# The last 96 rows of w_down: one load on 16 DMA engines, or on 8 with 12 rows each

## The chip, the cores and the metric

The kernel runs on one NeuronCore of a Trainium2 chip, in one launch. The metric is the device time of one execution in microseconds. The core has TensorE (PE, with its weight loads shown apart as PEld), VectorE (DVE), ScalarE (ACT), GpSimd (POOL) and SyncE (SP), and 16 DMA engines that carry all loads and stores.

## What is computed

A decode step of one token for a batch of B = 2, hidden size D = 512, in float32. The normalised input goes through an attention over the last W = 2048 positions of a cache, and through a bilinear feed-forward part; both are added to the input.

```python
xn = _layernorm(x)                                   # x: (2, 1, 512)
q = (xn @ wq) -> (2, 32, 1, 128)
k, v = k_cache[:, :, Sk - W:], v_cache[:, :, Sk - W:]  # (2, 32, 2048, 128) each
p = softmax(q k^T * 128 ** -0.5)
A = (p v) -> (2, 1, 4096) @ wo                       # wo: (4096, 512)
h = (xn @ w_gate) * (xn @ w_up)                      # F = 1376 columns
Bf = h @ w_down                                      # w_down: (1376, 512)
out = x + A + Bf
```

Almost all of the data is the cache: 32 heads with 2 MB of keys and 2 MB of values each. Every byte is used once.

## The kernel before, in words

**One stream of loads.** The host lays all large inputs out as one long array, `stream`, in the order in which the kernel wants them: keys and values of the heads, and between them the slices of wq, wo, w_gate, w_up and w_down. `blocks()` (from line 40) lists the loads in order, each as a list of fields with their widths; a load fills 128 partitions, each with one contiguous row. `pump()` (lines 148 to 171) issues them all from SP, in that order, into a ring of three large buffers called `step`; it stops when all three are held, and `done()` starts it again when the last field of a buffer has been used. So SP's queue has every large load of the kernel in one fixed order, and the DMA engines run through it.

**Heads.** For each head VectorE multiplies the keys by q (`products`) and adds them up (`sums`); GpSimd takes the maximum and the sum over the partitions; ScalarE takes the exponential; TensorE weighs the values (`pv`, `weigh`), transposes the result and multiplies it by wo (`project_o`), adding it up in a PSUM tile `acc`. Values run three heads behind keys.

**The feed-forward part.** w_gate and w_up come early, and h lies transposed in `hT`. w_down, 1376 rows, is cut into ten chunks of 128 rows and one rest of FR = 96 rows. The chunks are fields `wd` of the stream in four loads, `WD = [(0, 4), (4, 7), (7, 9), (9, 10)]`. The rest isn't in the stream: it is an input of its own, `wd_rest`, and its load is added as the very last of the list (line 142, with `at` None), into the same buffer as the last loads of the stream, on partitions 0 to 95 (line 168).

**The end.** After the last head's values the code calls `transpose(H - 1)`, `down(1)`, `project_o(H - 1)`, `down(2)`, `down(3)` and then the rest, each of the chunks as four matmuls of 128 columns into four row groups of `acc` (`accumulate`). In the profile a float32 matmul stands as two records, so a chunk is x8. Then VectorE adds x (`x_nat`, line 489, tile `o_out`), and SP stores 4 KB.

**Order.** `InOrder` (line 72) ties every instruction to the one before it on its engine, so that each engine runs in the order of the code. Since all calls of PE, DVE, ACT and SP go through it, the profile shows them with one line, L87; tiles tell them apart. `x_nat`, the input in the layout of the output, is loaded at the start from ScalarE's queue by two small loads of 4 rows of 512 bytes each.

Of the kernel before, what the change touches and what calls it, by code (L numbers as in the profile page):

```python
# [16 lines left out]
P = 128  # L17
B, D, H, DH, SK, F = 2, 512, 32, 128, 8192, 1376
# [5 lines left out]
NFC = F // P  # L24
FR = F - NFC * P
# [14 lines left out]
def blocks():  # L40

    def wd(n):
        return [("wd", i, D) for i in range(*WD[n])]

    def k(h):
        first = [("w", 1, CQ - NC * DH)] if h == 0 else []
        return [("k", h, CK)] + first + ([("wq", h, CP)] if h + HG < H else [])

    def v(h):
        return [("v", h, CK), ("wo", h, CO)]

    def gu(half):
        n = NC * (FH[half][1] - FH[half][0])
        return [("wg", half, n), ("wu", half, n)]

    units = []
    for h in range(LAG, H - 1):
        units += [k(h), v(h - LAG)]  # L60
    loads = [k(0), gu(0) + k(1), gu(1) + k(2), units[0] + units[1]]
    loads += [sum(units[i : i + 3], []) for i in range(2, len(units), 3)]
    loads += [k(H - 1) + v(H - 1 - LAG)]
    out = [(("q", 0), [("w", 0, NC * DH)])]
    out += [(("s", i), fields) for i, fields in enumerate(loads)]
    late, last = ("s", len(loads)), ("s", len(loads) + 1)
    out += [(late, v(H - 3)), (late, v(H - 2)), (last, wd(0)), (last, [("v0", H - 1, CK // 2)])]
    out += [(last, [("v1", H - 1, CK // 2), ("wo", H - 1, CO)])]
    return out + [(last, wd(n)) for n in range(1, len(WD))]
# [33 lines left out]
def kernel(  # L103
# [10 lines left out]
    pe, dve, act, sp = (InOrder(tc, e) for e in (nc.tensor, nc.vector, nc.scalar, nc.sync))  # L114
# [28 lines left out]
    tiles, used, left, got = {}, {}, {}, {}  # L143
# [4 lines left out]
    def pump():  # L148
        nonlocal held
        while todo:  # L150
            key, fields, at = todo[0]
            if key not in tiles:
                if key[0] == "q":
                    tiles[key] = const.tile([P, NC * DH], F32, name="wq0")
                elif held == BUFS:
                    return
                else:
                    held += 1
                    tiles[key] = steps.tile([P, STEP], F32, name="step")
                used[key] = 0  # L160
            todo.pop(0)
            c0 = used[key]
            for kind, i, w in fields:
                got[kind, i] = (tiles[key][:, used[key] : used[key] + w], key)
                used[key] += w
            c1 = used[key]
            if at is None:
                sp.dma_start(tiles[key][:FR, c0:c1], wd_rest)
            else:
                src = stream[at : at + P * (c1 - c0)].rearrange("(p i) -> p i", p=P)  # L170
                sp.dma_start(tiles[key][:, c0:c1], src)

    def done(kind, i):
        nonlocal held
        _, key = got.pop((kind, i))
        left[key] -= 1
        if left[key] == 0 and key[0] != "q":
            del tiles[key]
            held -= 1
            pump()  # L180

    pump()

    mean_w = const.tile([P, P], F32, name="mean_w")
# [309 lines left out]
def laid_out(x):  # L494


    import numpy as np

    a = x["A_x"].reshape(B, D)
    xs = a.reshape(B, P, NC).transpose(1, 0, 2).reshape(P, B * NC)  # L500
    picks = np.zeros((P, 4 * B), a.dtype)
    for b in range(B):
        for r in range(4):
            picks[4 * b + r :: 32, r * B + b] = 1.0
    cache = {
        kind: x[name][:, :, SK - W :, :].reshape(B, H, P, J * DH).transpose(1, 2, 0, 3)
        for kind, name in (("k", "A_k_cache"), ("v", "A_v_cache"))
    }
    wq = x["A_wq"].reshape(P, NC, H // HG, GC).transpose(2, 0, 1, 3)
    wo = x["A_wo"].reshape(H, P, D)  # L510
    gu = {
        kind: x[name].reshape(P, NC, F)
        for kind, name in (("wg", "B_w_gate"), ("wu", "B_w_up"))
    }
    wd = x["B_w_down"]

    def field(kind, i):
        if kind in ("k", "v"):
            return cache[kind][i].reshape(P, CK)
        if kind in ("v0", "v1"):  # L520
            return cache["v"][i].reshape(P, B, -1)[:, int(kind[1])]
        if kind == "w":
            return (wq[0][:, :, DH:] if i else wq[0][:, :, :DH]).reshape(P, -1)
        if kind == "wq":
            return wq[i // HG + 1][:, i % HG, :]
        if kind == "wo":
            return wo[i]
        if kind == "wd":
            return wd[i * P : (i + 1) * P]
        return gu[kind][:, :, FH[i][0] : FH[i][1]].reshape(P, -1)  # L530

    parts = [
        np.concatenate([field(kind, i) for kind, i, _ in fields], axis=1).ravel()
        for _, fields in blocks()
    ]
    return {
        "x": xs, "picks": picks, "x_rows": a.reshape(B, D // P, P),
        "stream": np.concatenate(parts), "wd_rest": wd[NFC * P :],
    }


# [29 lines left out]
```

## Time and profile before

| | us |
|---|---|
| median of 3 runs (380.22 to 380.51) | 380.46 |
| the profiled execution, its own time | 380.54 |
| its span, from the first to the last instruction | 378.4 |
| busy: PE / PEld / DVE / ACT / POOL | 260.7 / 93.1 / 294.4 / 63.9 / 25.4 |
| mean granted TensorE clock | 0.815 |

The profile is one execution. A row of a timeline is start, length, engine, line, operation, tiles, and in brackets the idle time of the engine before it and what ended it. SPq is SP's queue: a DMA stands there when it is issued, not when it lands. In a table of stretches the "DMA share" is the mean busy share of the 16 DMA engines; it can pass 1.00, as packets overlap a little.

### The profile page before, as it was taken

The numbers are of one execution on the slowest core, as the hardware profiler recorded it, in microseconds if no ns is written. First come the engines' busy times: TensorE is split into PE (matmuls) and PEld (weight loads), VectorE is DVE, ScalarE is ACT, GpSimd is POOL, SyncE is SP. The second block draws the span as 40 slices with busy tenths as digits, with TensorE's granted clock in tenths as the row PEclk, the third lists the DMA queues.
The fourth block names the chain that finished last, engine by engine and source line by source line (L and its number), as shares of the span: only waits on it lengthen the run. The fifth ranks groups of instructions, "written<-read, shape, count | busy, mean of one in ns | idle before, by whom it ended". The sixth has DMA issues, their size and how long they took to land.

```text
span 378.4 us, 3087 instructions
## 1 busy us (share of the span) xinstructions
PE 260.7 (69%) x1188; PEld 93.1 (25%) x1188; DVE 294.4 (78%) x145; ACT 63.9 (17%) x264; POOL 25.4 (7%) x78
## 2 busy tenths in 40 slices
PE   3939861746848875584885678487667847719996
PEld 3512220212212221221222122122212211204343
DVE  3739892996799499589949959994994999699920
ACT  1020020102102220201222021021112102212221
POOL 0000000000000000000000000000000010000000
PEclk9987995969876696978679588788867869668999
DMA  8999999999999999999999999999999999999994
GB/s 312 456 416 441 421 456 444 409 450 433 413 450 415 444 444 405 450 456 392 457 428 415 456 409 440 456 393 462 444 398 452 415 427 433 445 424 411 431 414 163
DMA packets 5049, 159.65 MB, mean 422 GB/s; under 512 B 828, under 2 KB 844, under 8 KB 1452
## 3 DMA queue, kind: packets, MB, share of 16 engines
q1 hardware_dynamic: 4732, 159.46, 98.2%
q8 instruction: 9, 0.15, 0.2%
q10 hardware_dynamic: 304, 0.01, 0.0%
q14 instruction: 4, 0.03, 0.0%
HBM read 159.46 MB, written 0.00 MB: 421 GB/s over the span
## 4 chain that ended last, share of the span: by engine, by line
DMA 60%; DVE 24%; PE 12%; ACT 2%; SPq 1%; issue 1%; POOL 0%; DVEq 0%
DMA step<-in_stream_dram 60%; DVE s L87 12%; DVE step L87 12%; PE o_ps L87 5%; PE q L87 3%; PE acc L87 2%; PE tr L87 1%; SPq L87 1%; ACT o_sb L87 1%; ACT oT L87 1%; DVE m L87 0%; ACT p L87 0%; DVE acc_sb L87 0%; DVE rec L87 0%; POOL mm L292 0%
## 5 line engine op out<-in xcount | busy, mean ns | idle before, releaser
L87 DVE TENSOR_TENSOR step<-step,q 128x4096 f32<-128x4096 f32 x31 | 136.6, 4407 | 56.9 <-DMA step<-in_stream_dram 51.5
L87 DVE TENSOR_REDUCE s<-step 128x32 f32<-128x4096 f32 x32 | 141.4, 4420 | 1.1
L87 PE MATMUL q<-step,xnb 128*128 128x512 f32 (+1 forms) x128 | 89.6, 846 | 60.4 <-DMA step<-in_stream_dram 60.4
L87 PE MATMUL o_ps<-step,p 128*8 128x512 f32 x512 | 82.1, 697 | 8.0 <-DMA step<-in_stream_dram 7.8
L87 PEld LDWEIGHTS q<-step,xnb 128*128 128x128 f32 x128 | 31.3, 267 | 115.4 <-DMA step<-in_stream_dram 57.0
L87 PE MATMUL tr<-pick,o_sb 128*128 128x2 f32 x256 | 33.7, 254 | 24.8 <-ACT o_sb L87 24.7
L87 PE MATMUL acc<-step,oT 128*17 128x512 f32 (+1 forms) x100 | 38.3, 538 | 13.4 <-ACT oT L87 13.4
L87 PEld LDWEIGHTS tr<-pick,o_sb 128*128 128x128 f32 x256 | 31.7, 193 | 53.2 <-ACT o_sb L87 52.5
L87 ACT COPY o_sb<-o_ps 128x512 f32<-128x512 f32 x33 | 19.2, 583 | 108.8 <-PE o_ps L87 108.8
L87 ACT ACTIVATE nm<-mm 128x2 f32<-128x2 f32 x32 | 6.5, 203 | 152.8 <-POOL mm L292 152.8
L292 POOL PARTITION_ALL_REDUCE mm<-m x32 | 11.4, 355 | 286.5 <-DVE rec L87 186.9
L87 PEld LDWEIGHTS o_ps<-step,p 128*8 128x8 f32 x512 | 13.6, 95 | 68.3 <-issue 58.0
L87 ACT ACTIVATE oT<-tr,rec 128x1 f32<-128x1 f32 x64 | 13.2, 258 | 38.0 <-PE tr L87 38.0
L87 ACT ACTIVATE p<-s,nm 128x16 f32<-128x16 f32 x64 | 19.2, 300 | 1.0
L308 POOL PARTITION_ALL_REDUCE sum<-rs x32 | 12.8, 399 | 41.2 <-ACT p L87 41.2
L87 PE MATMUL o_ps<-step,xn 128*2 128x512 f32 (+1 forms) x48 | 13.0, 597 | 0.0
L87 ACT ACTIVATION_READ_ACCUMULATOR p<-s,nm 128x1 f32 x64 | 11.9, 187 | 0.0
L87 PE MATMUL q<-xnb,mean_w 128*128 128x512 f32 (+1 forms) x24 | 11.9, 584 | 0.0
L87 DVE TENSOR_TENSOR o_out<-acc,x_nat 128x128 f32<-128x128 f32 x1 | 0.3, 292 | 11.2 <-PE acc L87 11.2
L87 PEld LDWEIGHTS acc<-step,oT 128*17 128x17 f32 x100 | 4.1, 98 | 18.1 <-ACT oT L87 15.1
L87 DVE TENSOR_TENSOR step<-step,tr 128x4096 f32<-128x4096 f32 x1 | 4.4, 4421 | 4.5 <-DMA step<-in_stream_dram 4.5
L87 DVE TENSOR_REDUCE m<-s 128x2 f32<-128x32 f32 x32 | 5.9, 186 | 1.1
(39 smaller groups left out, 38.8 us busy)
## 6 DMA issues: line engine op xcount, KB each, us to landing
step<-in_stream_dram SPq DMA_DIRECT2D x16, 6912.0 KB, 31.5
step<-in_stream_dram SPq DMA_DIRECT2D x2, 6400.0 KB, 28.1
step<-in_stream_dram SPq DMA_DIRECT2D x1, 6656.0 KB, 29.2
step<-in_stream_dram SPq DMA_DIRECT2D x1, 4608.0 KB, 26.7
step<-in_stream_dram SPq DMA_DIRECT2D x2, 2304.0 KB
step<-in_stream_dram SPq DMA_DIRECT2D x1, 4352.0 KB, 24.6
step<-in_stream_dram SPq DMA_DIRECT2D x1, 3712.0 KB, 33.9
step<-in_stream_dram SPq DMA_DIRECT2D x1, 3072.0 KB, 10.7
```

What stands on the lines that cost most here:

```text
L87: made = call(*args, **kwargs)
L292: nc.gpsimd.partition_all_reduce(mm, m, P, bass_isa.ReduceOp.max)
L308: nc.gpsimd.partition_all_reduce(sum_t[h], rs, P, bass_isa.ReduceOp.add)
```

## The change

The host stores the 96 rows in another order: as 12 by 8 rows and not as 96, so that row 12 e + j of the rest lies at place 8 j + e. The kernel reads this array with its two outer sizes swapped back, 8 by 12 by 512, so that the rows reach the same partitions as before. What the DMA writes is unchanged, 96 partitions of 2 KB; what it reads has 8 as its outermost size and not 96. The load is meant to go to 8 DMA engines, 12 rows each, where it went to 16 with 6 rows each.

```diff
             if at is None:
-                sp.dma_start(tiles[key][:FR, c0:c1], wd_rest)
+                sp.dma_start(tiles[key][:FR, c0:c1], wd_rest.rearrange("j e n -> e j n"))
             else:
...
         "x": xs, "picks": picks, "x_rows": a.reshape(B, D // P, P),
-        "stream": np.concatenate(parts), "wd_rest": wd[NFC * P :],
+        "stream": np.concatenate(parts), "wd_rest": wd[NFC * P :].reshape(8, -1, D).transpose(1, 0, 2),
     }
```

The instructions of PE, DVE, ACT and POOL are the same in both kernels, in the same order. On SP one DMA of 19 rows differs, this one.

## The prediction

> **What bounds the kernel now.** I read the page from its top first: the busy shares of the DMA engines, the queues, the chain that ended last.
>
> ```profile
> span 378.4 us, 3087 instructions
> ...
> DMA  8999999999999999999999999999999999999994
> ...
> DMA packets 5049, 159.65 MB, mean 422 GB/s; under 512 B 828, under 2 KB 844, under 8 KB 1452
> ## 3 DMA queue, kind: packets, MB, share of 16 engines
> q1 hardware_dynamic: 4732, 159.46, 98.2%
> q8 instruction: 9, 0.15, 0.2%
> q10 hardware_dynamic: 304, 0.01, 0.0%
> ...
> DMA 60%; DVE 24%; PE 12%; ACT 2%; SPq 1%; issue 1%; POOL 0%; DVEq 0%
> ```
>
> The 16 DMA engines are busy for 98.2% of the span with the loads of q1, and the chain lies 60% on them. So the kernel ends when its last bytes are in, and only the last slice, where the DMA digit falls from 9 to 4, is not full. The edit is about the very last load, so I go to the end: first the chain there, then what TensorE's weight loads (PEld) wait for.
>
> ```profile
> 354.95 19.48 DMA step<-in_stream_dram
> 374.44 0.04 issue
> 374.48 0.84 PE acc L87 x16
> 375.32 0.02 issue
> 375.35 0.29 DVE o_out L87
> ```
>
> ```profile
> 373.60 0.45 PEld L87 LDWEIGHTS acc<-step,hT 128*17 128x17 f32 x16
> 373.71 1.57 PE L87 MATMUL acc<-step,hT 128*17 128x128 f32 x32
> 374.48 0.13 PEld L87 LDWEIGHTS acc<-step,hT 128*17 128x17 f32 x8 [0.43 <-DMA step<-in_stream_dram]
> 374.86 0.13 PEld L87 LDWEIGHTS acc<-step,hT 96*17 96x17 f32 x8 [0.25 <-DMA step<-in_wd_rest_dram]
> 375.35 0.29 DVE L87 TENSOR_TENSOR o_out<-acc,x_nat 128x128 f32<-128x128 f32 x1 [11.21 <-PE acc L87]
> 375.67 0.69 SPq L87 DMA_DIRECT2D out_dram<-o_out  x1
> ```
>
> Two waits end the kernel, one behind the other. TensorE idles 0.43 us for the tenth 128-row chunk of w_down (the last load of the stream) and starts it at 374.48. Then it idles 0.25 us for the 96 rows and starts on them at 374.86. From there all is in series: sum at 375.35, store issued at 375.67, end at 378.4. Whatever moves the landing of the 96 rows later moves the end by as much; whatever moves it earlier helps only until the wait before it is the last.
>
> The question is then how the 16 engines come to their end. The stretches of the last 5 us show it (columns: stretch, its length, busy of the five engines, clock, DMA share, GB/s):
>
> ```profile
> 369.00:370.00 1.00, 0.96 (x3) 0.13 (x1) 0.00 (x0) 0.00 (x0) 0.00 (x0) 1.00 1.04 426
> ...
> 371.00:371.50 0.50, 0.50 (x6) 0.30 (x2) 0.00 (x0) 0.29 (x1) 0.00 (x0) 1.00 0.94 356
> 371.50:372.00 0.50, 0.42 (x4) 0.16 (x2) 0.00 (x0) 0.29 (x1) 0.00 (x0) 1.00 0.85 250
> 372.00:372.50 0.50, 0.50 (x6) 0.50 (x6) 0.00 (x0) 0.00 (x0) 0.00 (x0) 1.00 0.79 283
> 372.50:373.00 0.50, 0.50 (x12) 0.48 (x15) 0.00 (x0) 0.07 (x1) 0.00 (x0) 1.00 0.70 246
> 373.00:373.25 0.25, 0.25 (x16) 0.25 (x12) 0.00 (x0) 0.25 (x2) 0.00 (x0) 1.00 0.68 197
> 373.25:373.50 0.25, 0.25 (x18) 0.25 (x13) 0.00 (x0) 0.10 (x1) 0.00 (x0) 1.00 0.31 82
> 373.50:373.75 0.25, 0.25 (x20) 0.25 (x14) 0.00 (x0) 0.00 (x0) 0.00 (x0) 1.00 0.27 82
> 373.75:374.00 0.25, 0.25 (x20) 0.25 (x12) 0.00 (x0) 0.00 (x0) 0.00 (x0) 1.00 0.41 115
> 374.00:374.25 0.25, 0.25 (x13) 0.05 (x4) 0.00 (x0) 0.00 (x0) 0.00 (x0) 1.00 0.08 16
> ```
>
> The engines do not end together. At 371 the share leaves 1.00; at 373.25 to 373.75 it is 0.31 and 0.27, that is 5 and 4 engines of 16; after 374.0 it is 0.08, one engine. The spread from first to last is 3 us, five times what one engine spends on its 6 rows. So **which engine is last** decides the sign of this change, not how many engines share the load.
>
> No view prints the engines one by one, but the trace's packet records have start, length and size, and each engine's packets follow one another to a few ns, so they can be chained. The 16 chains of q1 begin their last semaphore write at 371.32, 371.41, 371.62, 372.36, 372.42, 373.08, 373.09, five between 373.31 and 373.41, 373.81, 373.92, 374.01 and 374.36, which is what the shares above count. Followed back to the start, four chains carry the 512-byte packets of the two x_nat loads, the same four both times. These four end at 372.36, 373.33, 374.01 and 374.36: **the two last of all are among them**. A chain falls behind by 0.7 to 1.5 us whenever an instruction fetch (q8, q14) takes its engine; that is what spreads them.
>
> **The change part by part.**
>
> *The issue on SP.* Same place in the order, one instruction for one.
>
> ```profile
> 343.02 12.36 SPq L87 DMA_DIRECT2D step<-in_stream_dram  x8
> 356.50 0.34 SPq L87 DMA_DIRECT2D step<-in_wd_rest_dram  x1
> ```
>
> ```profile
> step<-in_wd_rest_dram SPq DMA_DIRECT2D x1, 192.0 KB
> x_nat<-in_x_rows_dram ACTq DMA_DIRECT2D x2, 2.0 KB
> ```
>
> The load is issued at 356.50 in 0.34 us, 17 us before its first byte could move, and SP has nothing behind it until the store at 375.67. Were the issue several times as long, nothing would wait: 0.
>
> *The instructions of the other engines.* The order of PE, DVE, ACT and POOL is the same, row for row. The layout of the rows in DRAM is made before the run: 0.
>
> *The transfer.* 192 KB on 16 engines is 12 KB each, 6 rows of 2 KB; on 8 it is 24 KB, 12 rows. Eight engines get 6 packets more, eight lose all 6. Price of 6 packets, from two rows. With all engines at work (369 to 370) 426 GB/s over 16 engines is 26.6 GB/s, 77 ns for 2 KB: 0.46 us. In the tail (373.50 to 373.75) 82 GB/s over 0.27 x 16 = 4.3 engines is 19 GB/s, 108 ns: 0.65 us. I take 0.55, the middle, since with eight engines idle the pace should lie between these. For an engine that holds none of the 96 rows any more, the same 0.46 to 0.65 us go.
>
> *The source.* 12 rows of an engine now lie 16 KB apart in DRAM where 6 lay together. The packets stay 2 KB. No row shows such a read at 2 KB; the bounds are no loss and twice the 77 ns for 12 packets, 0.9 us more. I take none, nearest to the rows at hand, where packets of 2 KB already come at the pace of large ones.
>
> *Which eight.* Both x_nat loads went to the same four engines, so the choice is fixed and not a rotation; I expect a load for eight to take these four and four more. From the trace alone I give that three chances in four, and half for the rest: 0.88 that the last engine is among the eight. The Trainium skill ("DMA: Bandwidth & Descriptors", "Why a DMA increments its semaphore by 16 and not by 1") states it outright: such a DMA goes on the largest number of engines up to 16 that divides both outer sizes, here 96 and 8, and on the lowest-numbered of them. By that rule the eight contain the four, and the sum is the one below; were they drawn freely, the first rival would hold in half of the cases. No row here numbers the engines.
>
> *Sum.* The last engine, at 374.36, gets 6 packets more: + 0.55 us. The landing that TensorE waits for moves with it, the 0.25 us wait becomes 0.80, and no work can cover it, since the only thing left on TensorE is this chunk. What frees up on the other eight (0.5 us each, earlier) lies ahead of nothing: their engines have nothing else to load, and the tenth chunk's rows stand ahead of the 96 rows on every engine, so its wait to 374.48 stays. The profiled execution took 380.54 us (span 378.4 and 2.1 around it); the median is 380.46, 0.08 less. Forecast 380.46 + 0.55 = **381.0 us**, + 0.14%.
>
> **The rivals.**
>
> *The last engine isn't one of the eight (ends faster).* Then the late engines are relieved by 0.46 to 0.65 us and the 96 rows land before the tenth chunk or with it. The gain ends where the wait in front becomes the last: the tenth chunk at 374.48, 0.13 us of weight loads, then the 96 rows at 374.61 and not at 374.86: - 0.25, 380.2 us. It needs all of the eight to be done by about 374.1 (the wait ends 0.5 us after the last chain's end, 374.36 to 374.86). For it: eleven engines are done by 373.25 and could take 6 packets more for nothing. Against it: the chains. It can't reach - 0.76 us, which is 0.2%.
>
> *An instruction fetch falls on one of the eight while it still loads (slower by more).* The nine packets of q8 are 0.15 MB, 16 KB each; 0.2% of 16 x 378.4 us over 9 is 1.3 us each. One of them runs in the last 2 us: the stretch 373.75 to 374.00 has 115 GB/s between stretches of 82 and 16. Now it meets an engine that is already done. With 12 rows, eight engines are busy 0.5 us longer, and one that is caught loses 1.0 to 1.5 us. From + 0.76 on it decides. Caught at 373.8 with a few packets left, that engine ends at about 375.1 to 375.6, + 0.8 to + 1.3: 381.5 us.
>
> *The load is not split as the change says.* If the 96 destination rows decide alone, it stays on 16 engines: 380.46. Against it: the source now has 8 as its outer size, and the x_nat loads with 4 rows ran on 4.
>
> **How the numbers follow.** 0.06 are for the load that isn't split; of the other 0.94, 0.88 have the last engine among the eight, 0.82, less a little for what I don't see: 0.80, shared by the forecast and the fetch. 0.2%, 0.76 us, is about what a measurement of this kernel can tell from no change. Forecast (last engine among the eight) 0.66, with a price of 0.35 to 1.0 us: the low end if the last packets run at 77 ns without the slow ones that this execution had, the high end if they run at the 150 to 160 ns of the last two packets of the last chain. Some two fifths of it, 0.26, lies over 0.76, as the strided source and the slow tail are both on that side, 0.40 within. Fetch 0.14, all slower. Faster rival 0.10 and unchanged 0.06, both within 0.2%. 0.04 stays for a gain that I don't see, such as another spread of the engines. So faster 0.04, same 0.56, slower 0.40. The range is 380.3 to 381.7: below lie most of the faster rival and the unseen gain, above it the worst of the fetch and of the strided source.
>
> **What would show it.** Right: the weight load for the 96 rows starts at 375.2 to 375.6 with an idle time of 0.7 to 1.1 us ahead of it that the load of the 96 rows ends, the tenth chunk still starts near 374.5, and from 374.0 on the stretches show a share of 0.05 to 0.15 for 0.5 us longer. The chain of waits ends on in_wd_rest. Wrong: both waits at their old place (not split), the 96 rows without a wait (the last engine relieved), or a wait over 1.3 us (a fetch or slow rows). The whole stands on the spread of the engines being the same in each execution: if fetches fall on other engines from run to run, the time would scatter by half a microsecond, where the three runs shown lie within 0.3 us.

## The result, and the profile after

| | median us | runs | ratio to before beside it (95%) |
|---|---|---|---|
| before | 380.27 (380.14 to 381.48) | 10 | |
| changed | 381.24 (380.68 to 382.31) | 10 | 1.0024 (1.0014 to 1.0034) |
| before, beside the second measurement | 380.30 (380.05 to 381.31) | 29 | |
| changed, measured again | 380.73 (380.50 to 381.44) | 11 | 1.0013 (1.0005 to 1.0022) |

Slower in both measurements, by 0.97 and by 0.43 us. In the first, nine of before's ten times lie within 0.4 us, while the changed kernel's ten spread over 1.6 us. Its profiled execution took 380.68 us (span 378.6), the lowest of its ten, so it shows less of the loss than the median has.

The end of the chain of waits of the changed kernel (start, length, what):

```profile
342.99 13.46 DMA step<-in_stream_dram
356.45 0.02 issue
356.46 18.65 DMA step<-in_wd_rest_dram
375.12 0.04 issue
375.16 0.46 PE acc L87 x8
375.62 0.02 issue
375.64 0.29 DVE o_out L87
```

The chain now ends on the load of the 96 rows, where that of before ended on the stream. It landed at 375.12 in this view. In the packet records its last packet ends at 374.66, and 0.5 us pass from there to TensorE's start, as in before (374.36 to 374.86). The weight loads that waited for a DMA come next: first the one of before for `v1`, the second half of the last head's values, then those of the changed kernel:

```profile
370.09 0.12 PEld L87 LDWEIGHTS o_ps<-step,p 128*8 128x8 f32 x8 [0.96 <-DMA step<-in_stream_dram]
```

```profile
370.56 0.12 PEld L87 LDWEIGHTS o_ps<-step,p 128*8 128x8 f32 x8 [0.76 <-DMA step<-in_stream_dram]
...
375.16 0.13 PEld L87 LDWEIGHTS acc<-step,hT 96*17 96x17 f32 x8 [0.43 <-DMA step<-in_wd_rest_dram]
```

The 96 rows start at 375.16 and not at 374.86, + 0.30 us. In this execution the values `v1` had come 0.47 us later than in before's (370.56 against 370.09), so TensorE reached the end later and no longer waited for the tenth chunk. From `v1` to the 96 rows TensorE has about 4.1 us of work (374.86 - 370.09 less the waits of 0.43 and 0.25 in before; 375.16 - 370.56 less 0.43 here, 4.17). So two things compete for the end: `v1` plus 4.1 us, and the landing of the 96 rows; the later one sets it. In before the landing came 0.68 us after the other.

The stretch of before behind the ones shown above, then the stretches of the changed kernel (DMA share and GB/s last):

```profile
374.25:374.50 0.25, 0.10 (x8) 0.02 (x6) 0.00 (x0) 0.00 (x0) 0.00 (x0) 1.00 0.00 0
```

```profile
373.25:373.50 0.25, 0.25 (x9) 0.23 (x13) 0.00 (x0) 0.10 (x1) 0.00 (x0) 1.00 0.33 115
373.50:373.75 0.25, 0.25 (x18) 0.25 (x14) 0.00 (x0) 0.25 (x2) 0.00 (x0) 1.00 0.30 115
373.75:374.00 0.25, 0.25 (x20) 0.24 (x12) 0.00 (x0) 0.06 (x1) 0.00 (x0) 1.00 0.26 98
374.00:374.25 0.25, 0.25 (x20) 0.25 (x12) 0.00 (x0) 0.00 (x0) 0.00 (x0) 1.00 0.15 49
374.25:374.50 0.25, 0.25 (x16) 0.25 (x12) 0.00 (x0) 0.00 (x0) 0.00 (x0) 1.00 0.11 41
374.50:374.75 0.25, 0.25 (x20) 0.23 (x10) 0.00 (x0) 0.00 (x0) 0.00 (x0) 1.00 0.07 25
```

In before the share was down to 0.08 at 374.0 and 0 after 374.25; here two engines (0.11 to 0.15) go on to 374.6. In the packet records these two end the tenth chunk at 373.55 and 373.67 and then move 12 packets each, at 84 ns mostly, to 374.60 and 374.66.

### The profile page after: what moved, and what is told of

The parts are those of the page before. It is cut to its first block, busy times and chain, and to the rows that moved or that the text cites. A ratio compares the mean times of both kernels' runs of the same rounds, so it can differ in the third digit from the quotient of the medians.

```text
span 378.6 us, 3087 instructions
## 1 busy us (share of the span) xinstructions
PE 263.4 (70%) x1188; PEld 94.0 (25%) x1188; DVE 294.4 (78%) x145; ACT 63.7 (17%) x264; POOL 25.4 (7%) x78
## 4 chain that ended last, share of the span: by engine, by line
DMA 56%; DVE 31%; PE 9%; ACT 2%; issue 1%; POOL 0%; SPq 0%; DVEq 0%
DMA step<-in_stream_dram 51%; DVE s L87 15%; DVE step L87 15%; DMA step<-in_wd_rest_dram 5%; PE o_ps L87 4%; PE acc L87 2%; PE q L87 2%; PE tr L87 1%; ACT o_sb L87 1%; ACT oT L87 1%; ACT p L87 1%; DVE m L87 1%; POOL mm L292 0%; DVE rec L87 0%; SPq L87 0%
## 5 line engine op out<-in xcount | busy, mean ns | idle before, releaser
L87 PE MATMUL q<-step,xnb 128*128 128x512 f32 (+1 forms) x128 | 91.1, 858 | 58.0 <-DMA step<-in_stream_dram 57.8
L87 PE MATMUL o_ps<-step,p 128*8 128x512 f32 x512 | 83.0, 706 | 7.1 <-DMA step<-in_stream_dram 7.1
```

The source lines that it names most:

```text
L87: made = call(*args, **kwargs)
```

## The experiments

The theory: the last of the 16 engines is among the eight, gets 6 packets more, and the end moves by them. The rivals: the strided source is the cost; a load that stands last on few engines is the cost; an instruction fetch that catches one of the eight is. Each row of a table compares with runs of before on the same chip.

### Strided source or number of engines

Stored 6 by 16, so the source is strided and 16 engines stay:

```diff
-wd[NFC * P :].reshape(8, -1, D).transpose(1, 0, 2)
+wd[NFC * P :].reshape(16, -1, D).transpose(1, 0, 2)
```

> The 96 rows are stored 6 by 16 and read as 16 by 6: rows of one engine lie 32 KB apart, and the load stays on 16 engines with 6 rows each. Theory (the late engines get 6 rows more): no change from before, 380.3 us within 0.3, the wait ahead of the 96 rows 0.2 to 0.4 us. Rival (a strided source makes each packet slower): half of the rows, so at least half of the loss, 380.8 us or more, and packets of the last load slower than 84 to 110 ns.

Eight engines with rows that lie together (one unused row behind each block of 12 keeps the 8 as a size of its own):

```diff
-sp.dma_start(tiles[key][:FR, c0:c1], wd_rest.rearrange("j e n -> e j n"))
+sp.dma_start(tiles[key][:FR, c0:c1], wd_rest[:, :12, :])
...
-wd[NFC * P :].reshape(8, -1, D).transpose(1, 0, 2)
+np.pad(wd[NFC * P :].reshape(8, 12, D), ((0, 0), (0, 1), (0, 0)))
```

> The 96 rows are stored as 8 blocks of 12 rows with one unused row behind each, so that the load goes to 8 engines, 12 rows each, from rows that lie together. Theory (12 rows on engines that are late): as the changed kernel, 381.2 us within 0.4, and single times spread over more than 1 us. Rival (the strided source is the cost): as before, 380.3 us.

And the changed kernel itself once more:

> The changed kernel itself, beside the three others on the same chip. If rows that lie apart cost nothing: 380.8 us, as with the 8 blocks of rows that lie together (380.78). If they do on 8 engines: 381.2 us, as first measured.

| | median us | before | ratio (95%) |
|---|---|---|---|
| 16 engines, strided | 380.40 | 380.28 | 0.9999 (0.9989 to 1.0009) |
| 8 engines, together | 380.78 | 380.28 | 1.0010 (1.0001 to 1.0019) |
| 8 engines, strided (the change, again) | 380.73 | 380.30 | 1.0013 (1.0005 to 1.0022) |

The strided source costs nothing that these runs can tell apart (0.1%, 0.4 us), on 16 engines or on 8; the eight engines cost 0.43 to 0.50 us either way. The rival falls. Two expectations were not met to the letter: the second kernel's 380.78 lies just under 381.2 less 0.4, and the first kernel's wait of 0.2 to 0.4 us can't be read, since in its profiled execution (380.96 us) `v1` came at 371.00 and TensorE waited neither for the tenth chunk nor for the 96 rows. The waits of the kernel with the rows together, then those of the changed kernel's second profile:

```profile
374.61 0.13 PEld L87 LDWEIGHTS acc<-step,hT 128*17 128x17 f32 x8 [0.52 <-DMA step<-in_stream_dram]
375.54 0.13 PEld L87 LDWEIGHTS acc<-step,hT 96*17 96x17 f32 x8 [0.80 <-DMA step<-in_wd_rest_dram]
```

```profile
374.47 0.13 PEld L87 LDWEIGHTS acc<-step,hT 128*17 128x17 f32 x8 [0.56 <-DMA step<-in_stream_dram]
375.26 0.13 PEld L87 LDWEIGHTS acc<-step,hT 96*17 96x17 f32 x8 [0.66 <-DMA step<-in_wd_rest_dram]
```

This is the picture that the prediction drew: the tenth chunk at 374.5 as in before, and the wait behind it grown from 0.25 to 0.80 and 0.66 us.

### More and fewer packets

Four engines with 24 rows:

```diff
-wd[NFC * P :].reshape(8, -1, D).transpose(1, 0, 2)
+wd[NFC * P :].reshape(4, -1, D).transpose(1, 0, 2)
```

> The 96 rows are stored 24 by 4 and read as 4 by 24: 4 engines with 24 rows each. Theory: 24 packets of 84 ns are 2.0 us on the last engine where 12 are 1.0, so the changed kernel's 381.2 + 1.0 = 382.2 us if a late engine is among the four, as the chains of before have it, and the idle time ahead of the 96 rows is 1.2 to 1.8 us. Rival (the late engines are not among those that a smaller load takes; the loss has another cause): 381.2 us or less.

381.31 us (before 380.28; ratio 1.0024, 1.0015 to 1.0033): + 1.03, twice the loss of eight engines but not the + 1.9 expected. By its time the run lies nearer to the rival's 381.2 or less than to the theory's 382.2.

```profile
375.73 0.13 PEld L87 LDWEIGHTS acc<-step,hT 96*17 96x17 f32 x8 [1.38 <-DMA step<-in_wd_rest_dram]
```

The wait is in the range, 1.38 us. The last engine moved its 24 packets in 2.07 us (373.16 to 375.23 in the packet records), so the price per packet is as expected. What the expectation missed is where it started: this engine had ended the stream at 373.16, not at 373.72 as the last one of before, and the engine that ended the stream last here, at 373.46, is not one of the four. The last engine of all is not always among four of the sixteen, and the more are drawn the likelier it is. The four chains that carry the x_nat packets can be followed to the end, and all four have 24 packets, so a smaller load does take the same engines. The Trainium skill ("DMA: Bandwidth & Descriptors", "Why a DMA increments its semaphore by 16 and not by 1") has the lowest-numbered engines taken; the trace agrees as far as both loads run on the same four, and no record numbers the engines.

The load left out, the tenth chunk's rows in its place (the output lacks the 96 rows' part):

```diff
-    todo.append((todo[-1][0], [("wd", NFC, D)], None))
...
-    accumulate(hT[:FR, NFC % 4, NFC // 4, :], got["wd", NFC][0][:FR], last=True)
+    accumulate(hT[:FR, NFC % 4, NFC // 4, :], got["wd", NFC - 1][0][:FR], last=True)
```

> The load of the 96 rows is left out, and the last matmuls take the first 96 rows of the tenth chunk in their place, so the output lacks these rows' part. Theory: the tenth chunk's wait stands ahead of it and becomes the last, so all that is to be gained is the 0.25 us wait of before: 380.0 us within 0.2. Rival (the load's issue or its semaphore costs more than its packets): 379.6 us or less.

379.79 us (before 380.28; ratio 0.9984, 0.9974 to 0.9994): - 0.49 us, between both. Its profiled execution was the second slowest of its twelve, 380.28 us. The last wait for a load in it is the one for `v1`; TensorE waits for no other up to the last chunks (the second line):

```profile
370.49 0.12 PEld L87 LDWEIGHTS o_ps<-step,p 128*8 128x8 f32 x8 [0.76 <-DMA step<-in_stream_dram]
...
374.00 0.88 PEld L87 LDWEIGHTS acc<-step,hT 128*17 128x17 f32 x32
```

So in this execution the floor is `v1` plus TensorE's 4.1 us, and not the tenth chunk. With `v1` at 370.09, as in before, the same 4.17 us would put the last eight weight loads at 374.26 and not at 374.86, a gain of 0.6 (an estimate from these rows). The tenth chunk came in time: its last packet ended at 373.23 (373.72 in before), as its packets took 84 to 95 ns where in before they took 84 to 128. Why they run faster without the 96 rows, the runs don't show.

### Where the load stands

The load ahead of the last buffer's other loads, on 8 and on 16 engines:

```diff
-    todo.append((todo[-1][0], [("wd", NFC, D)], None))
+    n = next(i for i, t in enumerate(todo) if t[0] == todo[-1][0])
+    todo.insert(n, (todo[-1][0], [("wd", NFC, D)], None))
```

> The 8-engine load is issued ahead of the last buffer's other loads, some 5 MB before the end, and no longer last. Theory (each DMA engine works off its own bytes, and 24 KB more on eight of them make the late ones later wherever they stand): the tenth chunk of w_down is then what comes late, by about 0.5 us against the same early load on 16 engines: 380.9 us, 0.4 to 0.6 above that kernel. Rival (the loss comes from the very end, where only eight engines have work): it is hidden, and this kernel equals the 16-engine one with the early load, 380.4 us.

> Before, with the 16-engine load of the 96 rows issued ahead of the last buffer's other loads. Each engine carries the same bytes, the tenth chunk's rows are now the last: they land where the 96 rows landed, and the two last chunks follow each other on TensorE, 0.13 us more. Theory: 380.4 us, within 0.3 of before. Rival (a load that stands last costs something of its own): 380.0 us or less.

| | median us | before | ratio (95%) |
|---|---|---|---|
| 8 engines, early | 381.93 | 380.30 | 1.0038 (1.0026 to 1.0050) |
| 16 engines, early | 381.15 | 380.30 | 1.0020 (1.0012 to 1.0029) |

Against each other, eight engines cost 0.78 us more than sixteen although the load no longer stands last, so the rival that hides it falls. The place is not the one that the theory named. TensorE takes the tenth chunk without a wait; what comes late is `v1`, here with eight engines:

```profile
372.03 0.12 PEld L87 LDWEIGHTS o_ps<-step,p 128*8 128x8 f32 x8 [0.96 <-DMA step<-in_stream_dram]
...
375.54 0.88 PEld L87 LDWEIGHTS acc<-step,hT 128*17 128x17 f32 x32
```

With sixteen it starts at 371.80 (below). That is 0.23 us of the 0.41 us by which the two profiled executions differ (381.93 and 381.52); the rest of the 0.78 stays open.

The 16-engine kernel was expected at 380.4 and lost 0.85 us. The cause stands in the stretches in which the early load passes, of the 16-engine kernel and then of before:

```profile
359.00:360.00 1.00, 1.00 (x12) 0.11 (x4) 1.00 (x1) 0.00 (x0) 0.00 (x0) 1.00 1.04 324
360.00:361.00 1.00, 1.00 (x6) 0.44 (x3) 1.00 (x1) 0.58 (x1) 0.00 (x0) 1.00 0.85 295
361.00:362.00 1.00, 1.00 (x10) 1.00 (x10) 0.96 (x2) 0.00 (x0) 0.00 (x0) 1.00 1.04 289
362.00:363.00 1.00, 1.00 (x6) 0.24 (x10) 0.16 (x2) 0.74 (x4) 0.35 (x1) 1.00 1.02 320
```

```profile
359.00:360.00 1.00, 1.00 (x7) 0.62 (x5) 1.00 (x1) 0.32 (x1) 0.00 (x0) 1.00 1.00 412
360.00:361.00 1.00, 1.00 (x7) 0.65 (x6) 1.00 (x1) 0.41 (x2) 0.00 (x0) 1.00 0.88 371
361.00:362.00 1.00, 0.82 (x10) 0.13 (x8) 0.93 (x3) 0.00 (x0) 0.00 (x0) 1.00 1.00 418
362.00:363.00 1.00, 0.97 (x12) 0.33 (x16) 0.00 (x0) 0.52 (x4) 0.35 (x1) 1.00 1.06 442
```

The engines are as busy, but move 1228 KB and not 1643 KB in the four stretches: 415 KB, about a microsecond at 420 GB/s, and `v1` behind it is late by more than its own 192 KB:

```profile
371.80 0.12 PEld L87 LDWEIGHTS o_ps<-step,p 128*8 128x8 f32 x8 [0.97 <-DMA step<-in_stream_dram]
```

371.80 against 370.09, 1.71 us: with 4.1 us of TensorE's work behind it, this is the end of that kernel. The packet records say which packets lose the time. The load itself takes 0.62 us on each engine. Of the 256 packets of 8 KB beside and behind it 73 take over 360 ns, where in before none does (314 ns as a rule), and with the 18 KB packets ahead of them this adds up to 0.9 us on each engine. Why they slow down isn't shown.

### The instruction fetch

28 tiny matmuls beside heads 4 to 17, so that TensorE's ninth fetch starts at 368.3 us (368.7 with 16 engines), and none between there and 375.9, in the changed kernel and in before:

```diff
         done("wq", h)
+        if 4 <= h < 18:
+            for _ in range(2):
+                pe.matmul(tr[0:8, 64:66], mean_w[:, 0:8], mean_w[:, 0:2], start=True, stop=True)
```

> The changed kernel with 28 tiny matmuls (8 by 2 into unused columns of tr, 112 instructions of TensorE) beside the heads 4 to 17, so that TensorE's ninth instruction fetch comes some 6 us earlier and none falls into the last 3 us. Theory of the fetch (the spread of the changed kernel, 380.7 to 382.3, is a fetch that catches one of the eight engines while it loads): the spread falls under 0.7 us and the median to about 380.8. Rival (the spread has another cause): spread over 1 us and the median of the changed kernel beside it.

> Before with the same 28 tiny matmuls that were added to the changed kernel in the run on the fetch, so TensorE's ninth fetch comes near 368 us here too. Theory (the loss is 6 packets more on a late engine, whatever the fetch does): the kernel with 8 engines took 380.99, this one is 0.4 to 0.7 below it, 380.3 to 380.6 us. Rival (moving the fetch into the stream's last 7 us is what cost it): 380.9 us or more.

| | median us (range) | before | ratio (95%) |
|---|---|---|---|
| 8 engines, fetch moved | 380.99 (380.72 to 382.16) | 380.30 | 1.0019 (1.0010 to 1.0028) |
| 16 engines, fetch moved | 381.19 (380.96 to 381.56) | 380.29 | 1.0023 (1.0012 to 1.0033) |

The spread of the 8-engine kernel stayed, 1.4 us: the fetch in the tail isn't shown as its cause. The second run came out as its rival said, 381.19 us and not 380.3 to 380.6: with the 28 matmuls, eight engines cost nothing more than sixteen. The waits of the 8-engine kernel, then of the 16-engine one:

```profile
370.73 0.12 PEld L87 LDWEIGHTS o_ps<-step,p 128*8 128x8 f32 x8 [1.66 <-DMA step<-in_stream_dram]
374.96 0.40 PEld L87 LDWEIGHTS acc<-step,hT 128*17 128x17 f32 x16 [0.25 <-DMA step<-in_stream_dram]
```

```profile
370.86 0.12 PEld L87 LDWEIGHTS o_ps<-step,p 128*8 128x8 f32 x8 [1.54 <-DMA step<-in_stream_dram]
375.37 0.13 PEld L87 LDWEIGHTS acc<-step,hT 96*17 96x17 f32 x8 [0.31 <-DMA step<-in_wd_rest_dram]
```

`v1` comes 0.64 and 0.77 us later than in before. In the 8-engine kernel TensorE waits 0.25 us for the tenth chunk and then not at all for the 96 rows (they are the second half of the x16); in the 16-engine kernel it waits 0.31 us for the 96 rows.

The packet records show why. The moved fetch holds its engine from 368.30 to 369.37 (8 engines) and from 368.66 to 369.73 (16). In both kernels this engine is then the last to end the tenth chunk, at 374.42 and 374.38, where the last one of before ended it at 373.72. With sixteen engines it has 6 packets more to move and ends at 374.88. With eight it is not one of the eight and has none, and the last of the eight ends at 374.73. So here the engine that ends the stream last isn't one of the eight, which is the condition of the prediction's first rival, and both kernels end at about the same time. The same fetch delays `v1`: in the 8-engine profile its engine's share of `v1` lands at 370.23, every other engine's by 369.53. The 28 matmuls weren't tried with the fetch left in place.

### What makes these engines late

Both kernels without the two x_nat loads (the output lacks x):

```diff
-    for b in range(B):
-        act.dma_start(x_nat[RB * b :: 32, :], x_rows[b])
```

> The changed kernel without the two x_nat loads, so the output lacks x. In the chains of before the four engines of these loads fall back by 0.2 to 0.8 us at the start and never make it up. Theory (late engines are late by such hits, and these four are among the eight): the eight are less late, and the loss against the 16-engine kernel without these loads falls to 0.1 to 0.4 us: about 380.4 us. Rival (the eight are late for other reasons): as the changed kernel, 380.7 to 381.2 us.

> Before without the two x_nat loads, so the output lacks x. Theory: the last engine of before was one of the four by 0.36 us, so some of that goes: 380.0 us within 0.2. Rival: 380.3 us, no change.

And before with x_nat as 128 more columns of the stream's first load, on all engines:

```diff
-    out = [(("q", 0), [("w", 0, NC * DH)])]
+    out = [(("q", 0), [("w", 0, NC * DH), ("xn", 0, P)])]
...
-    dve.tensor_tensor(o_out, acc_g, x_nat, op=ALU.add)
+    dve.tensor_tensor(o_out, acc_g, got["xn", 0][0], op=ALU.add)
```

> Before with x_nat as 128 more columns of the stream's first load, spread over all 16 engines, in place of the two small loads on four of them: 64 KB more in the stream, 0.15 us at 430 GB/s. Theory: gains what the kernel without these loads gains, less 0.15 us: 380.1 us, 0 to 0.3 below before. Rival (these loads don't set the last engine): 380.45 us, slower by the 64 KB.

| | median us | before | ratio (95%) |
|---|---|---|---|
| 8 engines, no x_nat loads | 380.73 | 380.29 | 1.0012 (1.0003 to 1.0021) |
| 16 engines, no x_nat loads | 380.19 | 380.29 | 1.0003 (0.9993 to 1.0012) |
| 16 engines, x_nat in the stream | 380.48 | 380.29 | 1.0007 (0.9997 to 1.0016) |

The loss between the first two is 0.54 us, as large as with the loads. The first and the third kernel came out as their rivals said; the second's 380.19 fits its theory (380.0 within 0.2) as well as no change. So these loads aren't what makes the late engines late, and spreading them gains nothing. The pair is the cleanest of all on the main point: waits with 16 engines, then with 8.

```profile
374.37 0.13 PEld L87 LDWEIGHTS acc<-step,hT 128*17 128x17 f32 x8 [0.41 <-DMA step<-in_stream_dram]
374.74 0.13 PEld L87 LDWEIGHTS acc<-step,hT 96*17 96x17 f32 x8 [0.24 <-DMA step<-in_wd_rest_dram]
```

```profile
374.47 0.13 PEld L87 LDWEIGHTS acc<-step,hT 128*17 128x17 f32 x8 [0.43 <-DMA step<-in_stream_dram]
375.39 0.13 PEld L87 LDWEIGHTS acc<-step,hT 96*17 96x17 f32 x8 [0.79 <-DMA step<-in_wd_rest_dram]
```

The 96 rows start 0.65 us later: 0.10 us stand in front of the tenth chunk, and 0.55 us are the last wait, 0.24 and 0.79 us.

What does make them late can be read from the packet records of thirteen of the profiles (all but the first of the changed kernel), since every engine works off the same sizes in the same order and its chain can be followed by them. In before, the engine that ends last is 1.24 us behind the first one at 26 us, 1.9 us after an instruction fetch of 8 KB at 98 us, and 2.56 us after another at 251 us; it keeps that to 367 us and loses 0.5 us more in the tail. An 8 KB fetch (queue q14) puts its engine back by 0.65 to 0.98 us and a 16 KB fetch (q8, TensorE's) by about 1.55 us, and no engine makes it up. The 8 KB fetches come at about 97, 102, 185 and 251 us and fall, in each of the ten profiles of kernels with x_nat loads on four engines, on three of these four. The engine that ends last is one of the three in twelve of the thirteen profiles; the exception is the 16-engine kernel with the moved fetch, where it is the engine that this fetch hit. Without the x_nat loads (16 engines) the engine that the fetches at 95 and 251 us hit is 1.17 us behind at 26 us and ends last all the same. What puts these engines back in the first 26 us isn't shown, and no run moved an 8 KB fetch.

No version here is faster than before with its output whole.

## Why the prediction was right, and where not

**Sign and place** hold, and the size in all comparisons but the first. Forecast + 0.55 us; measured + 0.97 and + 0.43 for the change, + 0.50 for its twin with the rows together, + 0.54 without the x_nat loads, against sixteen engines without them. The wait for the 96 rows, forecast to grow from 0.25 to 0.80, is 0.43, 0.66, 0.80 and 0.79 in four profiles; in the first of them the 96 rows start at 375.16, just ahead of the 375.2 to 375.6 that was named, and the tenth chunk isn't waited for. The first measurement is over 0.2% and the second under it; their intervals overlap (0.14 to 0.34% and 0.05 to 0.22%). Why the ten first runs lie higher and spread wider stays open.

**The price of 6 packets.** Taken as 0.55 between 77 and 108 ns a packet. The last engine takes 0.99, 1.18, 1.23 and 1.19 us for its 12 packets in the four profiles, where the last engine of before took 0.64 for 6 (the records' 373.72 to 374.36): + 0.35 to + 0.59. Most packets run at 84 ns, near the low end of the price; the rest are packets of 120 to 196 ns that some engines meet, as the last one of before did (164 and 149).

**Three readings that don't bear on the sum.** The first of the 96 rows' packets starts at 370.82, 14 us after the load's issue and not 17. By 373.25 seven engines are done and not eleven; twelve are by 373.41. A 16 KB fetch takes 1.0 to 1.1 us in the records and not 1.3, but with the slower packet behind it (2.5 and not 2.0 us for 54 KB) its engine loses about 1.55.

**The source.** Taken at nothing: right, 380.40 against 380.28.

**"No work can cover it"** failed. TensorE's own chain from `v1` was only 0.68 us behind in before. In the first profile after, `v1` came 0.47 us later, and of that execution the late landing cost only the wait of 0.43.

**The rivals.** The gain was bounded at 0.25 us by the wait for the tenth chunk; leaving the load out gained 0.49. The bound was read from one wait, and in the profile of that run this wait was gone too and TensorE's chain from `v1` was the floor; the bound should have been read from that chain. With the moved fetch the engine that ended the stream last was not one of the eight, and there the eight cost nothing, as this rival has it. The fetch on one of the eight, given 0.14, isn't borne out as the cause of the spread: moving it left the spread. That the load isn't split is excluded by the 12 packets of each chain.

**Why the engines are late.** The prediction gave two reasons. The fetches are borne out, by 0.65 to 1.55 us each. The four x_nat engines are late and do carry the smaller load (all four in the 4-engine kernel, all four among the eight in the kernel with the rows together), but not because of the x_nat loads: three of them are hit by the 8 KB fetches, and they fall back early on without these loads too. That the 8 KB fetches hit three of these four in each profile is what made one execution a good guide; the prediction did not know it, and so far it was lucky.

## What to carry to other kernels

A load that is spread over fewer engines moves the same bytes, but the end waits for the last engine: look at how the DMA share falls in the last microseconds, and price the extra packets on the engines that still run there. Then look for the chain that is next behind the landing, here one load's landing plus 4.1 us of TensorE: it bounds both what the change can cost and what it can gain. Which engine is last was settled long before the end here, by what it lost in the first 26 us and by instruction fetches that it never made up. Moving the load ahead of the others didn't help: it cost 0.85 us on sixteen engines and 1.63 on eight.

## Unexpected

A 192 KB load of 2 KB rows ahead of large loads made the stream itself slow: 289 to 324 GB/s over 4 us where before had 371 to 442, at about the same busy share, 0.85 us in all, while the same load at the end costs at most the 0.49 us that leaving it out gains. The 8 KB packets of the other loads lose most of it, 0.66 us on each engine. And 112 more instructions on TensorE, which has idle time, cost the 16-engine kernel 0.9 us: they moved one instruction fetch to 368.66, and the engine that it held ended last, at 374.88 and not at 374.36 as the last of before, with `v1` 0.77 us later.
